# Queueing later weight conversions behind the work at hand in an attention and two-layer-pair kernel

## The chip, the cores and the metric

One core of a Trainium2 chip runs the whole program. The metric is the device time of one execution in microseconds (us), as a median of several runs. TensorE (PE) does the matrix products, VectorE (DVE), ScalarE (ACT) and GpSimd (POOL) the elementwise work, and one DMA queue on SyncE (SP) issues all transfers. Each engine takes its own instructions in the order of the program.

## The reference

```
attn:  a = softmax(causal(q k^T / 8)); local = a v
       mem = (phi(q) M_prev) / (phi(q) z_prev + 1e-6), phi(x) = elu(x) + 1
       x = sigmoid(beta) mem + (1 - sigmoid(beta)) local     # 2304 tokens x 512
moe :  h = x w_in;  x = (h * cos(h)) w_out                   # 512 -> 2048 -> 512
moe2:  h = x w_in;  out = (h * tanh(softplus(h))) w_out      # 512 -> 2048 -> 512
```

Queries, keys and values are 4 x 8 x 576 x 64, and all data of the two feed-forward pairs come as 8-byte words (float64).

## The kernel before, in words

Every product of the two feed-forward pairs is made of three: each operand is split into a rounded high part H and a rest L, and H·H, H·L and L·H are added in PSUM. So each value that enters a product first costs a cast (`scaled`) and a subtraction.

The weights come as 8-byte words. `fetch` (L133) loads 512 of them for each partition into a tile `wst` (4 buffers); `to_f32` turns them into float32: a rescaling of the upper word (`scaled("ws")`, L129 when GpSimd does it), a conversion of the lower word on ScalarE (L140) and two shift-and-merge steps on VectorE (L141, L142). Then comes the cast (L125 on ScalarE, L129 on GpSimd) and the subtraction. A **conversion** below is all of this for one `wst`. The table `TURNS` says which engines take which kind of step in turn.

The stages, by the time of the profile:

1. **Attention** (0 to 380 us), with the first half of the first pair's weights converted beside it, and the first pair's first half (`ffn` with blocks of 256 tokens, 36 units) from about 130 us to 472 us. In its tail, after attention is over, `load_half` converts the second half of the first pair's weights: 16 conversions (`gb`).
2. **First pair, second half** (472 to 690 us): `ffn` with blocks of 512 tokens, again 36 units, which come in twos. For two units: L422 products into `h`; L376 and L377 (the argument of the cosine), L381 (sin on ScalarE, both units at once), L384 (h·cos), the cast of `g` and the subtraction L394 on GpSimd; one pair later the L481 products into `y`. At the end of a block L504 adds the partial sum from DRAM (`yp`, loaded by L503) and L505 stores it to `ysF`. Beside it `strassen_weights` converts the second pair's weights: 16 conversions for `w_in` with sums of sub-blocks (L533), their H and L parts (L537) and stores to `wsD`; then 16 for `w_out`, kept on chip as `wo`. `strassen_x` forms the sums of the first 768 tokens (`xr` to `xc`, stored in `xsD`).
3. **Second pair, by Strassen's scheme** (690 to 1081 us): 24 groups, three blocks of 768 tokens by eight slices `tl` of the hidden dimension. A group k makes seven products A11, S2, A12, S3, S1, A22, S4 (L625, six matmuls each) from seven `wq` tiles (10 buffers) and seven `xc` tiles into two PSUM banks; a copy of the first product (`x1`, L675, ScalarE) and sums (L638, VectorE) turn them into four outputs, each with Mish on ScalarE (L642), a cast and a subtraction (L645) into `g3`. The L656 products of group k-1 (36 matmuls into `y`) stand between the products of group k. In group 6 and 14 the sums for the next 768 tokens are started (`coming`).

The order on each engine is set by a scheduler that works from the order in which the code is traced and from its own estimates. `tc.issue_after(ins)` puts every instruction that is traced inside it, on `ins`'s engine, behind `ins` in that engine's order; it sets an order and adds no semaphore. Without it the scheduler may put a conversion for a later group ahead of work at hand.

## Time and profile before

| what | us |
|---|---|
| median of 3 runs | 1083.99 (1081.04 to 1084.61) |
| the profiled execution | 1082.9 |
| its span, first to last instruction | 1081.1 |
| TensorE busy | 1034.7 |
| VectorE / ScalarE / GpSimd busy | 555.2 / 506.3 / 469.9 |
| mean granted TensorE clock | 0.982 of full speed |

A row of the timeline gives the start, the length, engine, line, operation, tiles and number of matmuls, and in brackets how long the engine was idle before it and who ended that. The waits group such idle times by who ended them. A table by windows gives the busy time of each engine in a stretch, the granted clock (1.00 is 2.4 GHz, 0.50 is 1.2 GHz) and the DMA engines' share.

### The profile page before, as it was taken

What the parts mean: (1) busy time and instruction counts of PE and PEld (TensorE: products, weight loads), DVE (VectorE), ACT (ScalarE), POOL (GpSimd) and SP (SyncE); (2) the same over time, 40 slices, a digit from 0 to 9 for tenths busy, and PEclk for the clock granted to TensorE, in tenths of its full rate; (3) what the DMA queues carried; (4) which work ended last, traced back from release to release, by engine and by line L of the source; (5) the groups of instructions that cost most, each with busy time, mean ns of one, the idle gap of its engine ahead of it and who ended that gap; (6) DMA issues with size and microseconds to landing.
All of it is one profiled execution on the core that took longest, in us unless ns stands there. A gap on an engine that the chain in (4) does not pass through costs nothing.

```text
span 1081.1 us, 18069 instructions
## 1 busy us (share of the span) xinstructions
PE 1034.7 (96%) x6560; PEld 890.6 (82%) x6560; DVE 555.2 (51%) x1214; ACT 506.3 (47%) x1102; POOL 469.9 (43%) x469
## 2 busy tenths in 40 slices
PE   6988999999999999899999999889999999999998
PEld 3756788787878899898888778778988889888987
DVE  4699864545555469725767856672224222322221
ACT  5886675555555544315445444433235233432323
POOL 3489633333333257615777996461126111511111
PEclk8999999999999999899999999889999999999999
DMA  7467323323221195414677795983436434454431
GB/s 258 163 224 244 123 90 102 119 88 95 86 75 54 43 340 189 156 47 145 219 285 301 254 341 203 394 307 117 125 111 219 117 110 135 127 173 120 118 88 59
DMA packets 88712, 177.36 MB, mean 164 GB/s; under 512 B 8240, under 2 KB 29232, under 8 KB 87600
## 3 DMA queue, kind: packets, MB, share of 16 engines
q1 hardware_dynamic: 88624, 176.21, 48.6%
q8 instruction: 52, 0.85, 0.3%
q14 instruction: 36, 0.29, 0.1%
HBM read 132.40 MB, written 43.78 MB: 163 GB/s over the span
## 4 chain that ended last, share of the span: by engine, by line
PE 77%; DMA 6%; POOL 5%; DVE 5%; ACT 3%; issue 3%; SPq 0%; ACTq 0%; DVEq 0%; POOLq 0%
PE y L656 18%; PE h L625 15%; PE h L422 15%; PE y L481 15%; PE o L333 4%; PE tp L306 3%; PE sp L247 3%; DVE wst L141 2%; PE o L322 1%; PE mp L286 1%; DVE wst L142 1%; DMA qd<-in_qT_dram 1%; DMA wq<-wsD 1%; POOL at L274 1%; POOL wst L129 1%
## 5 line engine op out<-in xcount | busy, mean ns | idle before, releaser
L481 PE MATMUL y<-g,w 128*128 128x256 f32 (+1 forms) x1344 | 226.4, 323 | 16.0 <-POOL g L394 7.0
L481 PEld LDWEIGHTS y<-g,w 128*128 128x128 f32 x1344 | 195.5, 196 | 43.8 <-issue 9.1
L656 PE MATMUL y<-wo,g 128*128 128x512 f32 x864 | 219.5, 395 | 4.1 <-ACT g L125 4.1
L422 PE MATMUL h<-xbH,w 128*128 128x256 f32 (+1 forms) x896 | 206.8, 317 | 0.0
L625 PE MATMUL h<-xc,wq 128*128 128x384 f32 x1008 | 197.2, 338 | 1.6 <-DMA wq<-wsD 1.0
L625 PEld LDWEIGHTS h<-xc,wq 128*128 128x128 f32 x1008 | 180.5, 189 | 12.4 <-DMA wq<-wsD 1.4
L656 PEld LDWEIGHTS y<-wo,g 128*128 128x128 f32 x864 | 161.9, 189 | 32.4 <-ACT g L125 4.4
L638 DVE TENSOR_TENSOR us<-h,us 128x384 f32<-128x384 f32 x120 | 66.8, 556 | 217.9 <-PE h L625 195.1
L645 POOL TENSOR_TENSOR g<-us,g 128x384 fp32r<-128x384 f32 x48 | 49.5, 1032 | 267.9 <-ACT g L125 253.8
L422 PEld LDWEIGHTS h<-xbH,w 128*128 128x128 f32 x896 | 151.0, 191 | 12.5 <-issue 1.0
L274 POOL TENSOR_SCALAR at<-at,sm,omg 128x128 f32<-128x128 f32 (+2 forms) x144 | 102.7, 723 | 128.3 <-DVE sm L272 109.7
L394 POOL TENSOR_TENSOR g<-u,g 128x512 fp32r<-128x512 f32 x72 | 102.5, 1439 | 126.5 <-DVE g L127 53.4
L422 PE MATMUL h<-xbL,w 128*128 128x256 f32 (+1 forms) x448 | 141.0, 315 | 0.0
L376 ACT ACTIVATE u<-h 128x512 int32<-128x512 f32 x72 | 42.4, 593 | 104.3 <-PE h L422 100.7
L422 PEld LDWEIGHTS h<-xbL,w 128*128 128x128 f32 x448 | 85.5, 191 | 5.4 <-issue 0.3
L252 ACT ACTIVATE at<-at,mn 128x128 f32<-128x128 f32 (+3 forms) x128 | 70.9, 555 | 27.1 <-DVE mn L249 25.6
L642 ACT ACTIVATE us<-us 128x384 f32<-128x384 f32 x72 | 37.7, 524 | 88.8 <-DVE us L638 88.7
L129 POOL TENSOR_SCALAR wst<-wst 128x512 f32<-128x512 f32 x64 | 52.7, 825 | 49.4 <-DMA wst<-in_w1i_dram 24.5
L141 DVE SCALAR_TENSOR_TENSOR wst<-wst 128x512 int32<-128x512 int32 x64 | 66.1, 1040 | 10.8 <-POOL wst L129 10.7
L377 DVE SCALAR_TENSOR_TENSOR u<-u,h 128x512 f32<-128x512 int32 x72 | 48.5, 680 | 43.2 <-ACT u L376 43.1
L142 DVE SCALAR_TENSOR_TENSOR wst<-wst 128x512 int32<-128x512 int32 x64 | 69.2, 1090 | 0.6
L306 PE MATMUL tp<-ident,at 128*128 128x128 f32 x384 | 62.6, 283 | 6.7 <-POOL at L274 5.5
(99 smaller groups left out, 1320.1 us busy)
## 6 DMA issues: line engine op xcount, KB each, us to landing
wq<-wsD SPq DMA_DIRECT2D x168, 256.0 KB, 3.0
wsD<-ws SPq DMA_DIRECT2D x8, 1792.0 KB, 7.8
wst<-in_w1i_dram SPq DMA_DIRECT2D x16, 512.0 KB, 4.7
wst<-in_w1o_dram SPq DMA_DIRECT2D x16, 512.0 KB, 5.6
wst<-in_w2i_dram SPq DMA_DIRECT2D x16, 512.0 KB, 4.5
wst<-in_w2o_dram SPq DMA_DIRECT2D x16, 512.0 KB, 6.0
xsD<-xc SPq DMA_DIRECT2D x7, 768.0 KB, 5.4
xc<-xsD SPq DMA_DIRECT2D x7, 768.0 KB, 9.0
```

Source lines behind the costliest of these rows:

```text
L129: eng.tensor_scalar(dst, src, scale, 1.0, ALU.mult, ALU.mult)
L141: nc.vector.scalar_tensor_tensor(lo, hi, -(1 << 31), lo, ALU.bitwise_and, ALU.bitwise_or)
L142: nc.vector.scalar_tensor_tensor(lo, hi, 3, lo, ALU.logical_shift_left, ALU.bitwise_or)
L252: marks["act"] = nc.scalar.activation(at[:, :N], at[:, :N], AF.Exp, bias=mn[:, j:j + 1], scale=-1.0, accum_out=sm[:, j:j + 1]).ins
L274: turn_of("sc", b == 0).tensor_scalar(at[:, :N], at[:, :N], sm[:, j:j + 1], gates[j], ALU.mult, ALU.mult)
L306: nc.tensor.transpose(tp[:, c:c + P], at[:, c:c + P], ident)
L394: turn_of(kind).tensor_tensor(gL, g, gH.bitcast(F32), ALU.subtract)
L422: nc.tensor.matmul(h[:, a * T:(a + 1) * T], w_[:, c, f0:f0 + P], x_[c], start=m == 0, stop=m == 3 * NC - 1)
L481: nc.tensor.matmul(y[e // per][:, cols], w_[:, f, es], g_, start=fst and m == 0 and e % per == 0, stop=lst and m == 2, skip_group_check=True)
L625: nc.tensor.matmul(b, w[:, wl, c], x[:, xl, c], start=first and m == 0, stop=m == 5, skip_group_check=True)
L638: nc.vector.tensor_tensor(c, b, x, ALU.add)
L656: nc.tensor.matmul(y[t], g[:, gl, t * P:(t + 1) * P], w_, start=tl == 0 and last == 0 and m == 0, stop=tl == ng - 1 and last == 1 and m == ...
```

## The change

Four edits that belong together, all in the second half of the program:

- **Tail of the first half, and the second half of the first pair.** The 16 conversions of `gb` come one for two steps from the start (before: all of the first six steps, then every second), each behind the last `marks["cos"]` (L384, VectorE) and the last sin (L381, ScalarE).
- **Fewer conversions of the second pair beside the first.** One for every fourth step rather than every third, so 1 of the 16 `w_out` conversions is done when Strassen's stage begins, where before it were 7 or more; in that stage `made_c` asks for 2k + 4 rather than 2k + 6.
- **In Strassen's stage** conversions and the sums for later tokens are traced under `behind()`, that is behind the last Mish (ScalarE), the last sum (VectorE), the last GpSimd subtraction and the last `wq` load (SP). The first group's `wq` loads are interleaved with the `xc` loads.
- **Engines.** The second pair's rescaling (`"ws2"`) and all its casts (`"wh2"`) go to ScalarE; before, GpSimd did all rescalings and half of the casts. The subtraction of the sums of tokens (`"x3l"`) goes to GpSimd and VectorE in turn.

```diff
-    wh="ap", aT="av", yl="p", ml="vp", y0="v", y1="a", aD="v", y3="a", x3l="p", x3d="v", ws4="p",
+    wh="ap", aT="av", yl="p", ml="vp", y0="v", y1="a", aD="v", y3="a", x3l="pv", x3d="v", ws4="p", ws2="a", wh2="a",
...
+    def load_w(tl, n):
+        t = wk.tile([P, 2, 2, P], F32R, tag="wq", name="wq", bufs=BUFS["wq"])
+        marks["s"] = nc.sync.dma_start(t.rearrange("p l c f -> p (l c f)").bitcast(F32), wsD[tl, :, SLOT[n]]).ins
+        return t
+
+    def load_sums(x, w):
         for n in PROD:
+            w[n] = load_w(0, n)
             x[n] = wk.tile([P, 2, 2, TS], F32R, tag="xc", name="xc", bufs=BUFS["xc"])
...
+    def behind():
+        es = ExitStack()
+        for e in "avps":
+            if e in marks:
+                es.enter_context(tc.issue_after(marks[e]))
+        return es
...
-            next(coming, None)
+            with behind():
+                next(coming, None)
...
-            if i < 2 * AHEAD or i % 2 == 0:
-                done_b = next(gb, done_b)
+            if i % 2 == 0:
+                with tc.issue_after(marks["cos"]), tc.issue_after(last_sin[0]):
+                    done_b = next(gb, done_b)
...
             while done_b < min(4 * ((i + 2) // 4 + 1), 4 * NTL) - 1:
-                done_b = next(gb)
+                with tc.issue_after(marks["cos"]), tc.issue_after(last_sin[0]):
+                    done_b = next(gb)
...
-            if i % 3 == 1:
+            if i % 4 == 1:
                 with tc.issue_after(marks["cos"]), tc.issue_after(last_sin[0]):
                     made_c = next(gc, made_c)
...
-        for k in strassen_ffn(b_pools[0], wo2, xs):
-            while made_c < min(2 * k + 6, DFF // P):
-                made_c = next(gc)
+        for k in strassen_ffn(b_pools[0], wo2, xs, w0):
+            while made_c < min(2 * k + 4, DFF // P):
+                with behind():
+                    made_c = next(gc)
```

How it moves instructions, at three places. VectorE in the tail of the first half, before, from the cosine products of two units (27 and 28, L384) to the next two's; `wst` is a conversion in work, `g` what the L481 products wait for:

```order
L384 TENSOR_TENSOR u_5292<-h_5303,u_5292 128x512
L178 TENSOR_TENSOR w112_4924<-wst_5295,w102_4923 128x512
L127 CAST g_5332<-u_5292 128x512
L141 SCALAR_TENSOR_TENSOR wst_5365<-wst_5365 128x512
L127 CAST g_5336<-u_5292 128x512
L142 SCALAR_TENSOR_TENSOR wst_5365<-wst_5365 128x512
L141 SCALAR_TENSOR_TENSOR wst_5429<-wst_5429 128x512
L142 SCALAR_TENSOR_TENSOR wst_5429<-wst_5429 128x512
L377 SCALAR_TENSOR_TENSOR u_5422<-u_5422,h_5397 128x512
L178 TENSOR_TENSOR w132_4926<-wst_5429,w122_4925 128x512
L141 SCALAR_TENSOR_TENSOR wst_5497<-wst_5497 128x512
L142 SCALAR_TENSOR_TENSOR wst_5497<-wst_5497 128x512
```

The same two units with the change:

```order
L384 TENSOR_TENSOR u_5268<-h_5279,u_5268 128x512
L141 SCALAR_TENSOR_TENSOR wst_5137<-wst_5137 128x512
L127 CAST g_5308<-u_5268 128x512
L141 SCALAR_TENSOR_TENSOR wst_5205<-wst_5205 128x512
L127 CAST g_5312<-u_5268 128x512
L142 SCALAR_TENSOR_TENSOR wst_5137<-wst_5137 128x512
L142 SCALAR_TENSOR_TENSOR wst_5205<-wst_5205 128x512
L178 TENSOR_TENSOR w111_4920<-wst_5205,w101_4919 128x512
L377 SCALAR_TENSOR_TENSOR u_5398<-u_5398,h_5373 128x512
L377 SCALAR_TENSOR_TENSOR u_5398<-u_5398,h_5413 128x512
```

Two conversions stand between two pairs of units instead of four, and the two L377 of the next pair follow each other.

ScalarE from the last outputs of Strassen's group 0 to the first of group 1, before; `us_7827` is the copy `x1` of group 1, `us_7855` its first Mish, `xc_8641` a sum for the next 768 tokens:

```order
L642 ACTIVATE us_7799<-us_7799 128x384
L125 ACTIVATE g3_7802<-us_7799 128x384
L675 ACTIVATE us_7827<-h_7819 128x384
L140 ACTIVATE wst_8081<-wst_8081 128x512
L140 ACTIVATE wst_8089<-wst_8089 128x512
L125 ACTIVATE wo012_6012<-wst_8089 128x512
L642 ACTIVATE us_7855<-h_7819 128x384
L571 ACTIVATE xc_8641<-xt_8639 128x768
L125 ACTIVATE g3_7857<-us_7855 128x384
```

The same place with the change; L648 is the Mish and L681 the copy:

```order
L648 ACTIVATE us_7751<-us_7751 128x384
L125 ACTIVATE wst_7335<-wst_7335 128x512
L140 ACTIVATE wst_7335<-wst_7335 128x512
L125 ACTIVATE wst_7429<-wst_7429 128x512
L140 ACTIVATE wst_7429<-wst_7429 128x512
L125 ACTIVATE g3_7754<-us_7751 128x384
L125 ACTIVATE wst_7578<-wst_7578 128x512
L140 ACTIVATE wst_7578<-wst_7578 128x512
L681 ACTIVATE us_7803<-h_7795 128x384
L125 ACTIVATE wo01_5972<-wst_7335 128x512
L125 ACTIVATE wo02_5974<-wst_7429 128x512
L648 ACTIVATE us_7831<-h_7795 128x384
```

The sum for later tokens is gone from between Mish and cast, and six conversion steps stand ahead of the copy of group 1.

TensorE where the first pair ends, with the change; `xc_7478` and `wq_7476` are the operands of A11 of group 0, `g_7414` belongs to unit 70 and `g_7541` to unit 71 of 72:

```order
L481 MATMUL y_7553<-g_7414,w121_4921 128x256 x2
L481 MATMUL y_7553<-g_7414,w131_4922 128x256
L630 MATMUL h_7683<-xc_7478,wq_7476 128x384 x6
L481 MATMUL y_7552<-g_7541,w122_4925 128x256
L481 MATMUL y_7553<-g_7541,w122_4925 128x256
```

Before, all 48 L481 products of units 71 and 72 stood ahead of the first L625 product; now A11 of group 0 stands ahead of them, and most of S2 in their middle.

## Rows read from the trace of the kernel before

**Rows 1.** The page: the span, and TensorE's busy time.
```profile
span 1081.1 us, 18069 instructions
PE 1034.7 (96%) x6560; PEld 890.6 (82%) x6560; DVE 555.2 (51%) x1214; ACT 506.3 (47%) x1102; POOL 469.9 (43%) x469
```

**Rows 2.** Table by windows: length, busy us of each engine (instructions), clock, DMA share, GB/s.
```profile
430.00:452.00 22.00, 19.04 (x135) 18.54 (x134) 20.57 (x25) 8.82 (x13) 17.15 (x16) 0.84 0.50 158
...
600.00:660.00 60.00, 54.89 (x250) 44.59 (x249) 40.81 (x45) 25.79 (x40) 56.10 (x45) 1.00 0.79 288
...
724.00:1050.00 326.00, 325.46 (x1619) 292.66 (x1618) 86.42 (x152) 112.95 (x214) 74.93 (x60) 1.00 0.44 131
```

**Rows 3.** Waits of PE from 430 to 452 us: total us, times, longest.
```profile
PE y L481 <- DVE yp L127: 1.7, 1, 1.7
PE y L481 <- POOL g L394: 1.3, 1, 1.3
```

**Rows 4.** Waits of PE from 600 to 660 us.
```profile
PE y L481 <- POOL g L394: 5.1, 4, 1.9
```

**Rows 5.** Waits of PE from 660 to 724 us.
```profile
PE y L656 <- ACT g L125: 4.1, 1, 4.1
PE y L481 <- ACT g L125: 3.2, 1, 3.2
PE h L625 <- DMA wq<-wsD: 1.0, 1, 1.0
PE y L481 <- POOL g L394: 0.6, 1, 0.6
```

**Rows 6.** Timeline of PE: start, length, line, tiles, matmuls, idle before.
```profile
427.64 5.92 PE L481 MATMUL y<-g,w 128*128 128x256 f32 x48
...
443.41 7.70 PE L481 MATMUL y<-g,w 128*128 128x256 f32 x42 [1.68 <-DVE yp L127]
...
663.89 3.63 PE L481 MATMUL y<-g,w 128*128 128x512 f32 x15
...
682.39 8.16 PE L481 MATMUL y<-g,w 128*128 128x256 f32 x46 [0.61 <-POOL g L394]
...
716.28 2.93 PE L656 MATMUL y<-wo,g 128*128 128x512 f32 x6 [4.06 <-ACT g L125]
...
724.20 1.55 PE L656 MATMUL y<-wo,g 128*128 128x512 f32 x6
```

**Rows 7.** Groups of DVE from 486 to 690 us, by form: busy, mean ns.
```profile
L142 DVE SCALAR_TENSOR_TENSOR wst<-wst 128x512 int32<-128x512 int32 x25 | 32.4, 1313 | 0.3
L141 DVE SCALAR_TENSOR_TENSOR wst<-wst 128x512 int32<-128x512 int32 x25 | 30.1, 1219 | 3.4 <-POOL wst L129 3.4
```

**Rows 8.** Groups of POOL from 486 to 690 us, by form.
```profile
L394 POOL TENSOR_TENSOR g<-u,g 128x512 fp32r<-128x512 f32 x36 | 54.3, 1526 | 36.6 <-ACT g L125 33.0 <-issue 3.6
L129 POOL TENSOR_SCALAR wst<-wst 128x512 f32<-128x512 f32 x22 | 17.3, 790 | 14.6 <-DMA wst<-in_w2i_dram 9.4 <-DMA wst<-in_w2o_dram 3.7 <-DVE wst L142 1.3
```

**Rows 9.** Timeline of ACT from 655 to 735 us.
```profile
676.71 1.15 ACT L381 ACTIVATE u<-u,c_hpi 128x1024 f32<-128x1024 f32 x1 [2.73 <-DVE u L377]
...
678.43 1.28 ACT L798 ACT_TABLE_LOAD   x1
...
706.21 1.24 ACT L140 ACTIVATE wst<-wst 128x512 int32<-128x512 uint32 x2
```

**Rows 10.** Landing times of L503, the loads of yp.
```profile
DMA to landing us min/median/max: 2.9/4.6/10.0
```

**Rows 11.** Landing times of L603, the loads of xc.
```profile
DMA to landing us min/median/max: 4.4/9.0/12.8
```

**Rows 12.** Table by windows, the stretch of the saturated DMA engines.
```profile
676.00:712.00 36.00, 31.11 (x166) 28.26 (x164) 25.31 (x33) 15.85 (x27) 17.79 (x16) 0.91 1.02 394
```

**Rows 13.** Groups of ACT from 690 us on, by form.
```profile
L642 ACT ACTIVATE us<-us 128x384 f32<-128x384 f32 x72 | 37.7, 524 | 88.8 <-DVE us L638 88.7
```

**Rows 14.** Groups of DVE from 690 us on, by form.
```profile
L579 DVE TENSOR_TENSOR xt<-xr,xt 128x768 f32<-128x768 f32 x2 | 3.5, 1771 | 2.2 <-DMA xr<-ysF 2.2
```

More of the change, by code (lines that the diff above doesn't have):

```diff
@@ L134, in fetch, with to_f32 @@
         return st
-    def to_f32(st):
+    def to_f32(st, kind="ws"):
         lo, hi = st[:, :, 0], st[:, :, 1]
-        scaled("ws", hi.bitcast(F32), hi.bitcast(F32), REBIAS)
+        scaled(kind, hi.bitcast(F32), hi.bitcast(F32), REBIAS)
         nc.scalar.activation(lo, lo.bitcast(U32), AF.Copy, scale=LOW * 2.0 ** -29, bias=0.2495)
@@ L516, in ahead @@
                 raw[i + AHEAD] = fetch(srcs[i + AHEAD])
-            yield to_f32(raw.pop(i)) if i >= 0 else None
+            yield to_f32(raw.pop(i), "ws2") if i >= 0 else None
     def strassen_weights(win, wout):
@@ L535, in sums @@
             for k0, k1, t in ((0, 2, pc[1]), (2, 3, pc[0][:, 0:1]), (3, 7, sw)):
-                scaled("wh", ws[:, k0:k1, 0], t)
+                scaled("wh2", ws[:, k0:k1, 0], t)
                 turn_of("w2l").tensor_tensor(ws[:, k0:k1, 1], t, ws[:, k0:k1, 0].bitcast(F32), ALU.subtract)
@@ L551, in gen @@
                         dH, dL = tiles[n - n_in]
-                        scaled("wh", dH, t)
+                        scaled("wh2", dH, t)
                         turn_of("w3l").tensor_tensor(dL, t, dH.bitcast(F32), ALU.subtract)
@@ L597, in strassen_x @@
         halves("S4", b22)
-    def load_sums(x):
+    def load_w(tl, n):
[3 more added lines that the diff above has]
+    def load_sums(x, w):
         for n in PROD:
+            w[n] = load_w(0, n)
             x[n] = wk.tile([P, 2, 2, TS], F32R, tag="xc", name="xc", bufs=BUFS["xc"])
@@ L604, in load_sums, with strassen_ffn @@
             yield n
-    def strassen_ffn(pool, wo, xs):
+    def behind():
[4 more added lines that the diff above has]
+        return es
+    def strassen_ffn(pool, wo, xs, w):
         ng = DFF // (2 * P)
@@ L611, in strassen_ffn @@
         ys = {}
-        def load_w(k):
-            w = {}
-            for n in PROD:
-                t = wk.tile([P, 2, 2, P], F32R, tag="wq", name="wq", bufs=BUFS["wq"])
-                nc.sync.dma_start(t.rearrange("p l c f -> p (l c f)").bitcast(F32), wsD[groups[k][1], :, SLOT[n]])
-                w[n] = t
-            return w
         def product(b, x, w, first):
@@ L637, in add @@
             c = cell()
-            nc.vector.tensor_tensor(c, b, x, ALU.add)
+            marks['v'] = nc.vector.tensor_tensor(c, b, x, ALU.add).ins
             return c
         def act(src, dst):
-            nc.scalar.activation(dst, src, AF.Mish)
+            marks['a'] = nc.scalar.activation(dst, src, AF.Mish).ins
             g = wk.tile([P, 2, TS], F32R, tag="g3", name="g3", bufs=BUFS["g3"])
             scaled("mh", g[:, 0], dst)
-            turn_of("ml").tensor_tensor(g[:, 1], dst, g[:, 0].bitcast(F32), ALU.subtract)
+            ins = turn_of("ml").tensor_tensor(g[:, 1], dst, g[:, 0].bitcast(F32), ALU.subtract).ins
+            marks['p' if ins.engine == mybir.EngineType.Pool else 'v'] = ins
             return g
@@ L666, in strassen_ffn @@
         g = {}
-        w = load_w(0)
         for k in range(n + 1):
@@ L674, in strassen_ffn @@
                 x1 = cell()
-                nc.scalar.activation(x1, A, AF.Copy)
+                marks['a'] = nc.scalar.activation(x1, A, AF.Copy).ins
                 product(B, x["S2"], w["S2"], True)
@@ L701, in strassen_ffn @@
                 if k + 1 < n:
-                    w = load_w(k + 1)
+                    w = {n: load_w(groups[k + 1][1], n) for n in PROD}
                 if groups[k][1] == ng - 2 and k + 2 < n:
@@ L706, in strassen_ffn @@
                     coming = strassen_x(nt, xs[nt])
-                    next(coming)
+                    with behind():
+                        next(coming)
             if k > 0:
@@ L772, in attention_moe_moe_kernel @@
     gx = strassen_x(0, {}, True)
-    xs = {0: {}}
-    gl = load_sums(xs[0])
+    xs, w0 = {0: {}}, {}
+    gl = load_sums(xs[0], w0)
     with tc.issue_after(marks["sp"]):
@@ L799, in attention_moe_moe_kernel @@
     with tc.issue_after(table), tc.issue_after(marks[large[-2]]):
-        for k in strassen_ffn(b_pools[0], wo2, xs):
-            while made_c < min(2 * k + 6, DFF // P):
-                made_c = next(gc)
+        for k in strassen_ffn(b_pools[0], wo2, xs, w0):
+            while made_c < min(2 * k + 4, DFF // P):
+                with behind():
+                    made_c = next(gc)
 _OUTS = [((2304, 512), "float32")]
```

## The prediction

> **What bounds the kernel now.** First the page: TensorE is busy for 1034.7 of 1081.1 us [rows 1], so a gain can come only from the 46 us in which it stands, or from stretches in which it runs at half clock. Then the table by windows, to see where these lie. From 724 to 1050 us TensorE is busy for 325.46 of 326.00 [rows 2]: nothing is to be had there, and whatever the change queues there can only lose. Other windows with holes (attention, the last store) lie outside the change. So I read the waits of TensorE and its timeline in the three places before 724 us; the reader is to see who ended each wait, and what the first matmuls after it cost.
>
> The clock is granted at 1.00 of 2.4 GHz in full stretches and at 0.50 (1.2 GHz) for a while after a long hole. The timeline shows it as slower matmuls: 48 took 5.92 us ahead of the hole of 1.68, and 42 took 7.70 behind it [rows 6]. At 5.92 / 48 = 0.123 each, 42 would take 5.2, so the half clock cost 2.5. The 46 behind the hole of 0.61 (which follows one of 3.2 [rows 5]) took 8.16 instead of 5.7: again 2.5. The first six behind the hole of 4.06 took 2.93, where six later took 1.55; I give this place 2.5 too, an estimate by the other two. The holes of up to 1.9 at 600 to 660 us left the clock at 1.00 [rows 2, 4].
>
> The bill of the kernel before, in us:
> - **A**, tail of the first half, 430 to 452: 1.7 + 1.3 [rows 3] + 2.5 = 5.5.
> - **B**, first pair's second half, 600 to 660: 5.1 in four holes, all ended by GpSimd's subtraction [rows 4].
> - **C**, the last units of the first pair: 3.2 + 0.6 [rows 5] + 2.5 = 6.3; **D**, the wait for `wq`: 1.0 [rows 5].
> - **E**, first products of `y` in Strassen's stage: 4.1 [rows 5] + 2.5 = 6.6.
>
> Together 24.5. All else keeps its time.
>
> **A: fewer conversions for a pair of units.** VectorE is busy for 20.57 of 22.00 us [rows 2]: it is the bound there. A conversion costs it 1.22 + 1.31 = 2.53 [rows 7]; a pair of units lasts TensorE 96 × 0.123 = 11.8, so the window holds nearly two pairs. Two conversions fewer for each pair take 2 × 2 × 2.53 = 10.1 off 20.57. VectorE then has half its time free, and the cast of `g` comes in time. −5.5, all of it. The other end: if one hole of 1.3 stays, without a cold stretch, plus another as long, −2.9. No conversions come short later: sixteen, two for each pair, need eight pairs, and the eighteen pairs of the stage have them.
>
> **B: GpSimd.** It is busy for 56.10 of 60.00 us [rows 2]. It loses the 22 rescalings (17.3 us of the 204 from 486 to 690) [rows 8] and, with the casts, more; conversions are begun every fourth step and not every third. Of 60 us this frees 60 × 17.3 / 204 = 5.1 by the rescalings, and a quarter of the remaining conversion work. The subtraction needs 36 × 1.53 = 54.3 us of those 204, and it is what TensorE waits for. −5.1; the other end, half of it, −2.5, if bursts of casts and of `x3l` still stand ahead of a subtraction. What takes over, ScalarE, was busy for 25.79 of 60 [rows 2]; its new steps (0.62 each, half of the 1.24 for two) [rows 9] add two for each conversion.
>
> **C and D: the end of the first pair.** I count from the end of the last product of the second-last layer half, 663.89 + 3.63 = 667.5 on the old time [rows 6], as 0. Ahead of A11 of group 0 TensorE now has 96 matmuls, 11.8 us. Its operands and the last `g` come by this chain: the fourth L504 waits for its `yp`, which is loaded after the first store: 1.5 (an estimate: the store's share of the 4.6) + 4.6 [rows 10] = 6.1. Behind it come the add and two L377, some 2.1 on VectorE (an estimate, by the 1.2 to 1.3 of L141 and L142 [rows 7]), so 8.2. Then on ScalarE the sin 1.15, two conversion steps 1.24, the table load 1.28 and the cast 0.6 [rows 9]: 12.5, some 0.5 more for the handing over, 13. Then the subtraction 1.53 [rows 8]: 14.5. The `xc` loads are issued at some 8.6 and land 4.4 later at the least [rows 11], at 13.0. So TensorE waits 13.0 − 11.8, about 1.4 with the sums, and then 0.9 for the subtraction: 2.3. Neither is as long as the holes that brought the half clock. Then the DMA: seven `xc` of 0.79 MB and seven `wq` of 0.26 MB make 7.3 MB; at 394 GB/s, the rate of the saturated stretch [rows 12], that is 18.6 us, so that S4's operands are there at about 29, where TensorE wants them at 28: 1.0. Left are 3.3 of 7.3: −4.0. The ends: nothing gained (the chain takes the place of the old wait, cold stretch and all), and −7.3.
>
> Of the table load the Trainium skill, "ScalarE: Activation LUTs", section "What ACT_TABLE_LOAD costs", says that a drain of about 1.38 us goes with each load. The row has 1.28 for the load and shows no drain; by the page the last `g` would come 1.4 later and C and D would give −2.6 rather than −4.0. I keep to the row.
>
> **E: group 1 of Strassen's stage.** Before, TensorE waits 4.1 there for a `g` that stood on ScalarE behind copies, conversions and a sum for later tokens. Now the sum is gone, but six conversion steps stand between the last Mish of group 0 and the copy `x1` of group 1, as the order shows. A12 of group 1 needs `x1`. After the end of S4 of group 0: the sum 0.6 (estimate), the Mish 0.52 [rows 13], six steps 6 × 0.62 = 3.7 [rows 9], a cast and the copy, each like the Mish, 1.0: 5.8. TensorE has twelve matmuls of 384 in the meantime; at 3.63 / 15 = 0.242 for 512 [rows 6] that is 12 × 0.18 = 2.2. The hole is 3.6, of the length that brought the half clock: 3.6 + 2.5 = 6.1, against 6.6. −0.5: this is a stall that changes its place. The ends: −6.6, if GpSimd or DMA deliver these conversions so early that ScalarE does them during the waits of group 0; and +1. In group 2 the same chain has two steps (0.6 + 0.5 + 1.24 + 0.5 = 2.9) against TensorE's 9 × 0.24 + 2.2 = 4.4, and from group 3 on four steps (0.6 + 0.5 + 2.5 + 1.0 = 4.6) against 24 × 0.24 + 2.2 = 8.0: no holes.
>
> On these six steps the Trainium skill, same page and section, says that ACTIVATEs back to back overlap by about 93 ns. The row has 1.24 for two of 512 columns, which shows no overlap; by the page the six steps would take 0.5 less and the hole would be 3.1. I take the row.
>
> **F: group 6.** The sums for the next tokens (two L579 of 1.77 [rows 14], an L572, and two conversions of 2.53 [rows 7]) now all stand between the last sum of group 6 and the first of group 7 on VectorE: 3.5 + 1.5 (estimate) + 5.1 = 10.1, with the add 10.6 after S4 of group 6. TensorE has about 9.3 of work till then (an estimate: 30 matmuls of 512 and 12 of 384, 30 × 0.24 + 2.2). +1.3, between 0 and +6.5 (a hole of 4 with its cold stretch). Before, the window shows only 0.54 of holes in all.
>
> **Sum.** −5.5 − 5.1 − 4.0 − 0.5 + 1.3 = −13.8. The profiled execution took 1082.9, 1.1 below the median 1083.99. 1082.9 − 13.8 + 1.1 = 1070.2; I say **1070**.
>
> **Rivals.**
> 1. **ScalarE's queue holds nobody up** (E ends at its good end, C and D near theirs): the conversions are fetched early enough and ScalarE is idle in group 0. For it: ScalarE waits for the sums for most of this stage (88.8 us) [rows 13]. Against: the order is fixed, and DMA is saturated just then [rows 12], so the words come late. −17 to −24.5: **1059.5 to 1067**.
> 2. **GpSimd and VectorE stay late** (B −2.5, C and D 0 to −2, F +4): for it, the subtractions stand in GpSimd's queue behind casts in bursts, and the subtraction of the sums moves to it in part. Against: the 17.3 us that it loses. −4 to −11: **1073 to 1080**.
> 3. **The change doesn't do what it says**: fewer conversions early mean more late, each stall is only moved, 1080.7 to 1087, around **1083**. Against: TensorE has no free time in which a later engine is the bound except at the four places.
> 4. **Slower, by one mechanism**: A11 of group 0 now stands ahead of the last 48 L481 products, and TensorE takes its work in order. If the store lands in 10, `yp` in 10.0 [rows 10] and `xc` in 12.8 [rows 11], its operands come at 10.0 + 10.0 + 12.8 = 32.8, where before no product of the first pair waited for them. Then the hole is 32.8 − 11.8 = 21.0 and with 2.5 it is 23.5 in place of 7.3: +16.2, with the rest (−9.8) +6.4: **1090**. It decides from a landing at about 29, since 29 − 11.8 + 2.5 − 7.3 − 9.8 = +2.6; that takes every one of the loads at its slowest, while the medians give 4.6 and 9.0.
>
> **How the numbers follow.** Forecast, 1067 to 1073: 0.42. Rival 1: 0.20. Rival 2: 0.22. Rival 3: 0.09. Rival 4: 0.07. About 0.3%, 3.3 us, is what a measurement of this kernel can tell from no change. So faster (below 1080.7) has 0.42 + 0.20 + 0.22 = 0.84, the same 0.09, slower 0.07. The range is 1060 to 1081: it holds the forecast, rival 2 and nearly all of rival 1.
>
> **What the next profile would show.** A: no wait between L481 and its cast in the tail, VectorE half busy, clock 1.00 there. B: no waits of L481 for the L394 subtraction between 600 and 660, GpSimd some 45 of 60. C and D: a wait of A11 for `xc` or `wq` of 1 to 2 us, and a wait of S4 of about 1. E: a wait of a product of group 1 for a copy on ScalarE of about 3.6, with slow matmuls behind it, and ScalarE busy with conversions ahead of it. F: a wait of about 1 in group 7, by VectorE. Outside these places the busy share of TensorE stays as it is, and the mean clock is above 0.982. I am wrong if `xc` lands late (rival 4 or the bad end of C and D), if the copy of group 1 is in time (rival 1), or if GpSimd is still the bound of B.

## The result, and the profile after

The changed kernel takes 1068.1 us (median of 4 runs, 1066.67 to 1070.39); the kernel before takes 1083.55 over the runs beside it. The ratio is 0.9863, with an interval of 0.9838 to 0.9888. The forecast was 1070, in a range of 1060 to 1081. The profiled execution, at 1070.39 the longest of the four, has a span of 1068.6 us, against 1081.1 [rows 1]:

```profile
span 1068.6 us, 18074 instructions
...
PE 1031.4 (97%) x6560; PEld 888.7 (83%) x6560; DVE 559.0 (52%) x1224; ACT 532.5 (50%) x1154; POOL 417.5 (39%) x407
```

The stage ahead of the change also differs a little from one program to the next: the same matmul at 206 us starts up to 4 us earlier or later in the programs of this study. So I compare from that matmul to the last products of `y`. These are the two rows of the kernel before, from TensorE's timeline, and behind them the same two of the kernel after:

```profile
205.54 5.78 PE L481 MATMUL y<-g,w 128*128 128x256 f32 x46 [1.39 <-ACT aT L125]
...
1070.11 6.32 PE L656 MATMUL y<-wo,g 128*128 128x512 f32 x27
```

```profile
207.49 5.78 PE L481 MATMUL y<-g,w 128*128 128x256 f32 x46 [1.39 <-ACT aT L125]
...
1057.56 6.32 PE L663 MATMUL y<-wo,g 128*128 128x512 f32 x27
```

864.57 us became 850.07: 14.5 less, where the prediction had 13.8 (the medians differ by 15.45). The table by windows of the kernel after answers to [rows 2]; its columns are the length, the busy time of PE, PEld, DVE, ACT and POOL, the clock, the DMA share and GB/s:

```profile
430.00:452.00 22.00, 22.00 (x186) 22.00 (x185) 16.78 (x21) 8.07 (x13) 14.46 (x13) 1.00 0.40 120
600.00:660.00 60.00, 60.00 (x306) 51.39 (x305) 37.77 (x48) 31.99 (x50) 38.94 (x30) 1.00 0.78 280
724.00:1050.00 326.00, 321.50 (x1585) 288.90 (x1584) 114.56 (x176) 124.18 (x235) 76.10 (x57) 0.99 0.47 140
```

In the first two windows TensorE has no hole left and GpSimd, which was full in the second (56.10), is busy for 38.94. In the third, where there was nothing to gain, 4 us of holes are new. TensorE's timeline, with the idle time ahead of each row in brackets, has every hole above 0.3 us that remains in the stretches which the change touches:

```profile
667.76 1.28 PE L630 MATMUL h<-xc,wq 128*128 128x384 f32 x6 [0.46 <-DMA xc<-xsD]
...
683.40 1.28 PE L630 MATMUL h<-xc,wq 128*128 128x384 f32 x6 [0.96 <-DMA wq<-wsD]
685.36 1.31 PE L630 MATMUL h<-xc,wq 128*128 128x384 f32 x6 [0.67 <-DVE us L644]
687.26 1.28 PE L630 MATMUL h<-xc,wq 128*128 128x384 f32 x6 [0.60 <-DMA wq<-wsD]
690.05 2.29 PE L630 MATMUL h<-xc,wq 128*128 128x384 f32 x6 [1.50 <-ACT us L681]
692.13 2.17 PE L663 MATMUL y<-wo,g 128*128 128x512 f32 x6
...
797.33 4.21 PE L630 MATMUL h<-xc,wq 128*128 128x384 f32 x12 [4.23 <-DVE us L644]
801.33 2.18 PE L663 MATMUL y<-wo,g 128*128 128x512 f32 x6
```

The first row is A11 of group 0, the second S4 of group 0, then A11, S2 and A12 of group 1. The rows at 690.05, 692.13, 797.33 and 801.33 run at half clock: six of 384 take 2.29 rather than 1.28, twelve 4.21 rather than 2.27, six of 512 take 2.17 and 2.18 rather than 1.55.

The bill beside the prediction's, in us:

| place | before | forecast of the change | after: holes + half clock | change |
|---|---|---|---|---|
| A tail of the first half | 5.5 | −5.5 | 0 | −5.5 |
| B second half | 5.1 | −5.1 | 0 | −5.1 |
| C, D end of the first pair | 7.3 | −4.0 | 0.46 + 0.96 | −5.9 |
| E group 1 | 6.6 | −0.5 | 0.67 + 0.60 + 1.50 + 1.6 | −2.2 |
| F group 7 | 0 | +1.3 | 4.23 + 2.6 | +6.8 |
| sum | 24.5 | −13.8 | | −11.9 |

The table misses 2.6 of the 14.5. Most of it is that an idle time is shorter than the delay that goes with it. I compare the start of the same matmul in both traces. From ahead of A's two holes to behind them the kernel before loses 3.5 us, where the idle times add up to 2.95; the half clock behind them costs 2.5, as the prediction had it. The four holes of B, 5.1 us of idle time, go with 6.4 us. C, D and E together give 8.6 rather than 8.1, and F costs 0.4 less than the table says. The likely reason is the row of the last matmul ahead of a hole: a matmul of 256 by itself has a row of 0.28 to 0.35 us, while in a run the next one starts after 0.12, so that part of the delay counts as busy. No run tests this reading.

### The profile page after: what moved, and what is told of

Its sections match the earlier page's. It is cut to its first block, busy times and chain, and to the rows that moved or that the text cites. A ratio compares the mean times of both kernels' runs of the same rounds, so it can differ in the third digit from the quotient of the medians.

```text
span 1068.6 us, 18074 instructions
## 1 busy us (share of the span) xinstructions
PE 1031.4 (97%) x6560; PEld 888.7 (83%) x6560; DVE 559.0 (52%) x1224; ACT 532.5 (50%) x1154; POOL 417.5 (39%) x407
## 5 line engine op out<-in xcount | busy, mean ns | idle before, releaser
L481 PE MATMUL y<-g,w 128*128 128x256 f32 (+1 forms) x1344 | 219.8, 317 | 4.2 <-ACT aT L125 4.2
L481 PEld LDWEIGHTS y<-g,w 128*128 128x128 f32 x1344 | 191.0, 190 | 29.5 <-issue 9.1
L651 POOL TENSOR_TENSOR g<-us,g 128x384 fp32r<-128x384 f32 x48 | 51.9, 1080 | 289.1 <-ACT g L125 282.1
L644 DVE TENSOR_TENSOR us<-h,us 128x384 f32<-128x384 f32 x120 | 66.7, 556 | 175.1 <-PE h L630 174.5
L394 POOL TENSOR_TENSOR g<-u,g 128x512 fp32r<-128x512 f32 x72 | 105.5, 1481 | 123.8 <-DVE g L127 45.1
L648 ACT ACTIVATE us<-us 128x384 f32<-128x384 f32 x72 | 37.7, 524 | 102.0 <-DVE us L644 99.4
L142 DVE SCALAR_TENSOR_TENSOR wst<-wst 128x512 int32<-128x512 int32 x64 | 72.4, 1142 | 0.6
L377 DVE SCALAR_TENSOR_TENSOR u<-u,h 128x512 f32<-128x512 int32 x72 | 48.7, 681 | 43.5 <-ACT u L376 43.1
L333 PE MATMUL o<-aT,vt 128*64 128x128 f32 (+1 forms) x896 | 67.4, 276 | 2.0 <-ACT aT L125 2.0
L249 DVE CUSTOM_DVE_ANT_0 at<-sp,mask 128x128 f32<-128x128 f32 (+3 forms) x128 | 59.1, 482 | 19.4 <-PE sp L247 11.8
```

What stands on the lines that cost most here:

```text
L142: nc.vector.scalar_tensor_tensor(lo, hi, 3, lo, ALU.logical_shift_left, ALU.bitwise_or)
L249: nc.vector.tensor_tensor_reduce(at[:, :N], sp[:, :N], mask[:, SM - q0:SM - q0 + N], SSC, 3.0e38, ALU.add, ALU.min, mn[:, j:j + 1])
L333: marks["pe"] = nc.tensor.matmul(o[j * D:(j + 1) * D, :n], st["vt"][:kk, c, j * D:(j + 1) * D], a, start=False, stop=c == i, skip_group_ch ...
L394: turn_of(kind).tensor_tensor(gL, g, gH.bitcast(F32), ALU.subtract)
L481: nc.tensor.matmul(y[e // per][:, cols], w_[:, f, es], g_, start=fst and m == 0 and e % per == 0, stop=lst and m == 2, skip_group_check=True)
L644: marks['v'] = nc.vector.tensor_tensor(c, b, x, ALU.add).ins
```

## The experiments

Each kernel was timed beside the kernel before, and one execution of it was profiled. The first four make a part of the change alone, on the kernel before; the others undo or change a part in the changed kernel. Two parts were never run by themselves: the first `wq` loads between the `xc` loads, and `x3l` on GpSimd and VectorE in turn. What each of these two is worth is not known.

### The tail alone

Only the first of the two edits on the first pair's conversions, on the kernel before:

```diff
-            if i < 2 * AHEAD or i % 2 == 0:
-                done_b = next(gb, done_b)
+            if i % 2 == 0:
+                with tc.issue_after(marks["cos"]), tc.issue_after(last_sin[0]):
+                    done_b = next(gb, done_b)
```

> The kernel before with the edit of the tail of the first half alone (conversions for the second half of the first pair one for two steps, behind the last L384 and the last sin). Theory: the tail is bound by VectorE's four conversions for each pair of units, so the waits of L481 between 430 and 452 us (1.7 and 1.3) and the half clock behind them go, 5.5 us, and the other places keep their waits: ratio 0.995. Rival: the conversions that are now later burden the stage behind; then the waits of L481 for GpSimd (5.7 in all from 600 on) begin earlier and grow by 2 or more, and the ratio is 0.997 to 1.001.

1090.89, ratio 1.0066 (1.0047 to 1.0085): slower, a miss for the theory and beyond the rival. The tail's own waits are gone, but where the second half begins the timeline shows new ones, this one and two more at 493 and 495 us (0.86 and 1.30):

```profile
479.19 0.80 PE L481 MATMUL y<-g,w 128*128 128x256 f32 x2 [2.93 <-DVE g L127]
```

The conversions which the tail no longer makes come there, and since that code didn't yet put them behind, two L141 (2.37 us) stand ahead of the cast of `g`. At the start of Strassen's stage the waits grow too, from 5.1 us to 6.9. The change has a second edit for these conversions, which this kernel leaves out.

### Both edits on the first pair's conversions

```diff
             while done_b < min(4 * ((i + 2) // 4 + 1), 4 * NTL) - 1:
-                done_b = next(gb)
+                with tc.issue_after(marks["cos"]), tc.issue_after(last_sin[0]):
+                    done_b = next(gb)
```

> The kernel before with both halves of the edit on the conversions of the first pair: one for two steps and behind the last L384 and sin in the tail, and also those that are still open in the second half traced behind them (the run of the tail alone left these as before, and had waits of 2.9 and 3.1 us with half clock between 479 and 570). Theory: it was these later conversions, put ahead of work at hand, that cost what the tail gave; with them behind it, A's 5.5 is a net gain: the waits between 470 and 600 are gone and the ratio is 0.994 to 0.997. Rival: it is their mere amount beside the second half, whose GpSimd rescalings come on top of those for the second pair; then L394's waits stay above 5 from 470 on and the ratio is 1.001 or more.

1081.86, ratio 0.9989 (0.9972 to 1.0006): no difference that the interval shows. The waits at 479 to 495 are gone, but TensorE's waits between 470 and 700 us are now more than in the kernel before (14.6 us in place of 9.9). The two largest (total, times, longest):

```profile
PE y L481 <- POOL g L394: 5.7, 5, 1.6
PE y L481 <- DVE yp L504: 3.6, 2, 3.1
```

L394's share is what it was before (5.7); what is new is the waits for VectorE and a later `wq`. So both were partly right: A's 5.5 come free, and what comes later takes them back. That the put-off conversions are the cause of each of these waits is likely, not shown. Alone, this part is worth nothing that the interval shows.

### The change of engines alone

`ws2="a", wh2="a"` with the two calls that use them, on the kernel before.

> The kernel before with the change of engines for the second pair's weights alone (rescaling and all casts on ScalarE; the sums for later tokens stay on GpSimd). Theory: GpSimd is the bound between 600 and 660 us, so the waits of L481 for L394 there (5.1) are gone and GpSimd is busy for some 40 of the 60 us; A keeps its 5.5; E, the wait for ScalarE at the first products of group 0, grows from 4.1 by the two or more extra steps of 0.6 that ScalarE gets there, to 5 to 7: in all -2 to -4, ratio 0.996 to 0.998. Rival: it is the rate of the conversions that frees GpSimd; then more than 2.5 of the 5.1 stay and the ratio is 1.000 to 1.003.

1073.87, ratio 0.9916 (0.9898 to 0.9934), about 10 us: more than the theory gave it. The waits from 470 to 700 us, and below them from 700 on:

```profile
PE y L481 <- POOL g L394: 3.5, 5, 0.9
...
PE y L656 <- ACT g L125: 2.4, 1, 2.4
```

L394's waits fell from 5.7 to 3.5 with none above 0.94, and the 3.2 ahead of the last units to 1.0: the last `g` had been late through GpSimd too. The wait of E shrank from 4.1 to 2.4, where I had expected that ScalarE's extra steps make it longer. By the same matmuls in both traces, 4.0 us were won up to the end of the last full block (656 us in the kernel before) and 6.0 behind it, in C, D and E.

### The smaller count alone

`i % 4` for `i % 3` and `2 * k + 4` for `2 * k + 6`, on the kernel before.

> The kernel before with the smaller count of conversions alone (every fourth step beside the first pair; in Strassen's stage 2k+4 asked for rather than 2k+6). Theory: B shrinks from 5.1 to 2 to 3, since GpSimd loses a quarter of the conversions there; the last two conversions now stand in VectorE's queue beside the sums of group 6, so a wait of a product of group 7 for L638 appears, as in the changed kernel (4.2 and the half clock, 6.8 in all); E grows, since nothing is queued behind: net +2 to +8, ratio 1.002 to 1.007. Rival: the wait in group 7 comes from tracing behind the work at hand, not from the count; then there is none here and the ratio is 0.996 to 1.000.

1083.99, ratio 1.0004 (0.9993 to 1.0015): nothing. L394's waits were 4.4 in two, and a wait of 5.84 for VectorE (L638) stood at 719 us, in an early group. In group 7 there was none, as the rival had it: without being put behind, the last conversions are drawn into earlier groups. So the smaller count by itself doesn't bring the wait of F.

### The engines undone

The changed kernel with `ws2="p", wh2="ap"`.

> The changed kernel with the old engines for the second pair's weights: rescaling on GpSimd, casts on GpSimd and ScalarE in turn. Theory: L481 waits for L394 again between 500 and 690 us, 2 to 5 us in all (with the smaller count alone 4.4 were left, with the new engines alone 3.5), and A11 and the last g come later behind GpSimd's queue, 2 to 3; in return three steps fewer stand ahead of the copy of group 1, and E's wait of 1.5 and half clock go, 3: net +1 to +5, 1069 to 1073, ratio 0.987 to 0.991. Rival: with the smaller count GpSimd has room enough and E's gain is all that is seen: 1064 to 1067, ratio 0.982 to 0.985.

1078.3, ratio 0.9945 (0.9927 to 0.9963): 10 us lost, outside both expectations. TensorE's waits from 470 to 700 us, and below them from 700 to 830:

```profile
PE h L630 <- DMA wq<-wsD: 3.5, 1, 3.5
...
PE y L481 <- POOL g L394: 1.5, 3, 0.8
...
PE y L663 <- POOL wo L129: 2.5, 1, 2.5
```

L394 is the smaller part of what comes back (1.5). A11 of group 0 waits 3.5 for its first `wq`, whose load SP issued at 666.19 us and not at 660.33 (why it was issued later, these traces don't settle), and a product of `y` waits 2.5 for the cast of `wo` in GpSimd's queue. E's wait for the copy stays at 1.5, although only three conversion steps stand ahead of it now; and in group 7 TensorE waits 3.0 for a Mish and 1.9 for a cast, where the changed kernel waits 4.2. The profiled execution is the longest of six, 1080.5.

### The tail undone

The changed kernel with the old two edits on the first pair's conversions.

> The changed kernel with the old order of the first pair's conversions (all of the first six steps of the tail, then every second; those left over not put behind). Theory: A's waits of 1.3 and 1.7 and the half clock are back, 5.5, and the second half gains nothing, since it has no waits of L481 left: 1073.5, ratio 0.991. Rival: the conversions that are done earlier free VectorE and GpSimd for more of the second pair's, which helps the start of Strassen's stage: 1070 or less.

1073.59, ratio 0.9902 (0.9888 to 0.9917), 5.5 above the changed kernel, which is what A was priced at. The old holes (1.28 and 1.68) are back with the half clock:

```profile
443.44 7.88 PE L481 MATMUL y<-g,w 128*128 128x256 f32 x42 [1.68 <-DVE yp L127]
```

That it is 5.5 to the tenth is chance: by the same matmuls in both traces the tail loses 6.2, and F is smaller here (3.03 in place of 4.23). Within the change, then, A is a net gain; alone it was none. What makes the difference is probably the room that the engines' edit gives in the second half, where L394's waits are 0.28 us in all; the tail together with that edit alone was not run.

### No conversions in group 6

The changed kernel with one line changed, so that group 6 has sums for later tokens and no conversions:

```diff
-            while made_c < min(2 * k + 4, DFF // P):
+            while made_c < (4, 6, 8, 11, 14, 16)[min(k, 5)]:
```

> The changed kernel with one edit: the conversions asked for in Strassen's stage are 4, 6, 8, 11, 14, 16 after groups 0 to 5 rather than 2k+4, so that none is left for the end of group 6, where the sums for the next tokens begin. Theory: two conversions on VectorE (5.8 us from the first L141 to the last L142 in the changed kernel) stand between the last sum of group 6 and the first of group 7, so that sum comes some 6 us earlier, the wait of 4.2 in group 7 and its half clock (2.6) go, and the time is 1068.1 - 6.8 = 1061, ratio to the kernel before 0.980. Rival: the sums themselves are slowed by GpSimd's work beside them (an L572 took 1.78 on VectorE) and by the landing of xr (1.9 of waits); then a wait of 2 to 4 stays with its half clock, 1065 to 1068.

1066.99, ratio 0.9845 (0.9824 to 0.9866), 3.4 us less in the profiled span. The direction is the theory's, and the half clock in group 7 is gone; by the same matmuls some 5 us are won in that place. But the median's gain of 1.1 is within what the intervals (0.9838 to 0.9888 for the changed kernel) can't tell from none. The changed kernel was profiled in its longest execution; how large F is in the other three, no trace shows. In group 7 waits of 0.20, 0.78 and 0.36 are left, of which the longest:

```profile
794.22 2.37 PE L630 MATMUL h<-xc,wq 128*128 128x384 f32 x12 [0.78 <-DVE us L644]
```

VectorE's work there is still uneven: an L579 takes 2.60 beside GpSimd's L589 (787.42 to 789.26), where one took 0.96 just before.

```profile
787.48 2.60 DVE L579 TENSOR_TENSOR xt<-xr,xt 128x768 f32<-128x768 f32 x1
```

The changed kernel holds a second comparison. In its group 14 the sums for the last 768 tokens are put behind in the same way, and no conversions are left: in group 15 TensorE waits only 0.27, for a Mish, as it did before the change.

### The sums' GpSimd work on VectorE

The changed kernel with `x3l="v"` and L589 and L594 on VectorE, which also takes this work from GpSimd in the first pair's second half; the two conversions stay in group 6.

> The changed kernel with all elementwise work of the sums for later tokens that GpSimd does (L572, L589, L594) given to VectorE; the two conversions stay in VectorE's queue in group 6. In the changed kernel two L141 took 4.56 us there beside GpSimd's L589 and L572, and 0.69 each where GpSimd was idle. Theory (VectorE is slowed by GpSimd's work beside it): without that work L141, L142 and L572 take 0.7 to 1.0 each, the eleven instructions ahead of the first sum of group 7 make about 9.0 us, and the wait falls from 4.2 to 2 or less: F costs 2 to 4 rather than 6.8, ratio to the kernel before 0.982 to 0.985. Rival (it is only the length of the queue): one L589 and one or two L572 of 1.8 to 2.5 come on top of 13.6 us, the wait grows to 7 or more, ratio 0.989 or above.

1066.71, ratio 0.9852 (0.9839 to 0.9865), 5.0 less in the profiled span; by the medians the gain is 1.4, which the intervals don't tell from none either. VectorE has more instructions ahead of the first sum of group 7 than in the changed kernel, and is done sooner. The changed kernel, VectorE (the last row is that sum):

```profile
785.57 0.96 DVE L579 TENSOR_TENSOR xt<-xr 128x768 f32<-128x768 f32 x1 [1.25 <-DMA xr<-ysF]
...
787.60 0.96 DVE L579 TENSOR_TENSOR xt<-xr,xt 128x768 f32<-128x768 f32 x1 [0.60 <-DMA xr<-ysF]
788.47 1.78 DVE L572 TENSOR_TENSOR xc<-xr,xc 128x768 fp32r<-128x768 f32 x1
790.17 4.56 DVE L141 SCALAR_TENSOR_TENSOR wst<-wst 128x512 int32<-128x512 int32 x2
794.65 1.28 DVE L142 SCALAR_TENSOR_TENSOR wst<-wst 128x512 int32<-128x512 int32 x2
...
796.73 0.55 DVE L644 TENSOR_TENSOR us<-h,us 128x384 f32<-128x384 f32 x1
```

GpSimd's work beside it:

```profile
789.40 2.56 POOL L589 TENSOR_TENSOR xr<-xr 128x768 f32<-128x768 f32 x1
791.92 2.26 POOL L572 TENSOR_TENSOR xc<-xt,xc 128x768 fp32r<-128x768 f32 x1
```

The experiment, VectorE, where GpSimd had only one instruction, from 788.27 to 789.77:

```profile
788.21 2.11 DVE L141 SCALAR_TENSOR_TENSOR wst<-wst 128x512 int32<-128x512 int32 x2
...
793.19 0.54 DVE L644 TENSOR_TENSOR us<-h,us 128x384 f32<-128x384 f32 x1
```

The two L141 take 4.56 beside two GpSimd instructions, 2.11 beside one; one alone takes 0.69. The wait falls from 4.23 to 0.79 and the half clock goes. That is not all GpSimd's: `xr` landed earlier here, and the 1.85 us that VectorE waits for it in the changed kernel are gone. From the end of S4 the sum is ready 3.4 us sooner: 2.4 by the L141 and 1.9 by `xr`, less 0.9 for the added instructions with the shorter L572 counted in. So two things make F, the conversions in the queue and GpSimd's work beside them, and a late `xr` adds to it. No conversions there (the run before this one) is enough to end the half clock, and so is this run's lighter GpSimd with the earlier `xr`; what GpSimd's work is worth without the change of `xr` is read from the rows, not tested.

### Fewer conversions behind group 0

As the kernel with no conversions in group 6, but with 3, 5, 8, 11, 14, 16, so that two are put behind group 0 rather than three.

> The changed kernel with conversions asked for as 3, 5, 8, 11, 14, 16 after groups 0 to 5: none in group 6, and two rather than three after group 0, so that four ScalarE steps rather than six stand ahead of the copy of group 1. Theory: F as with 4, 6, 8, 11, 14, 16 (waits of 2.1 in all in place of 4.2 and the half clock), and the wait for the copy of group 1 falls from 1.5 to 2.0 to below 1, with no half clock behind it (1.6): 1064, ratio 0.982. Rival: E's copy does not wait for the steps but for A11's own end or for the clock; then the wait and the half clock stay and the time is that of the other, 1067.

1068.25, ratio 0.9867 (0.9854 to 0.9879): no gain, a miss. The wait for the copy is still 1.46 in group 1, and stands now in groups 2 and 3 too:

```profile
688.12 1.32 PE L630 MATMUL h<-xc,wq 128*128 128x384 f32 x6 [1.46 <-ACT us L681]
705.64 1.32 PE L630 MATMUL h<-xc,wq 128*128 128x384 f32 x6 [1.71 <-ACT us L681]
723.89 2.27 PE L630 MATMUL h<-xc,wq 128*128 128x384 f32 x6 [2.33 <-ACT us L681]
```

The last row is at half clock; in group 1 the half clock is gone. The conversions which group 0 is spared burden the next ones. In group 1 the copy does come sooner, 3.7 us after the start of group 0's last sum rather than 5.3, but TensorE has waited less on its way there (0.9 in place of 2.2) and is there sooner by nearly as much.

### Conversions not put behind

The changed kernel, with this alone undone:

```diff
             while made_c < min(2 * k + 4, DFF // P):
-                with behind():
-                    made_c = next(gc)
+                made_c = next(gc)
```

> The changed kernel, but the conversions of Strassen's stage are traced without being put behind the work at hand (the sums for later tokens still are). Theory: by the order the conversions then stand ahead of the Mish of group 0 on ScalarE and are over before group 6: the wait of 4.2 in group 7 goes (-5 to -7), and at the first outputs of group 0 a wait of a product of y for ScalarE is back, 2 to 5 us with the half clock, in place of E's 3.8: in all 1063 to 1068, ratio 0.981 to 0.985. Rival: the words land late since DMA is saturated, the Mish of group 0 waits for them, and the wait is 6 or more: ratio 0.986 or above.

1060.72, ratio 0.9797 (0.9784 to 0.9810): the fastest kernel here, 7.4 us below the changed one and better than both expectations. E and all but 0.8 of F are gone. TensorE's two largest waits from 660 to 800 us:

```profile
PE y L481 <- POOL g L394: 0.9, 1, 0.9
PE h L630 <- DVE us L644: 0.8, 2, 0.5
```

ScalarE's timeline shows where the conversions went: from 666 to 676 us, into the time in which, in the changed kernel, it waited 7.34 for TensorE.

```profile
666.33 0.68 ACT L125 ACTIVATE wst<-wst 128x512 f32<-128x512 f32 x1
...
675.54 0.68 ACT L125 ACTIVATE wst<-wst 128x512 f32<-128x512 f32 x1 [0.71 <-DMA wst<-in_w2o_dram]
```

And TensorE gets other work in its own order: products of `y` stand between those of group 0, and there is no wait for `wq` left in that group.

```profile
678.47 1.67 PE L663 MATMUL y<-wo,g 128*128 128x512 f32 x6
679.98 1.21 PE L630 MATMUL h<-xc,wq 128*128 128x384 f32 x6
681.02 0.86 PE L663 MATMUL y<-wo,g 128*128 128x512 f32 x3
```

### Nothing put behind in Strassen's stage

The same, and the sums for later tokens are not put behind either.

> The changed kernel with nothing put behind the work at hand in Strassen's stage: neither conversions (as in the run before this, 1060.7) nor the sums for later tokens. By the order, the sums of the next tokens are pulled forward on VectorE. Theory: the sums were what the tracing behind was good for; next to GpSimd an L579 or L572 takes 2 to 2.6 us on VectorE and on ScalarE an L571 0.8, so ahead of the work at hand they bring waits of 1 to 4 us in the first groups: 1063 to 1067, ratio 0.982 to 0.986. Rival: the scheduler puts them where the engines have room, as it did with the conversions: 1059 to 1061.5, ratio 0.978 to 0.981.

1066.24, ratio 0.9844 (0.9829 to 0.9860): the theory's range, 5.5 above the run before. TensorE waits for `wq` (0.99 and 1.33) and for a subtraction on VectorE. Behind that it runs at half clock: 18 matmuls take 4.96, where 18 took 3.37.

```profile
688.05 3.37 PE L630 MATMUL h<-xc,wq 128*128 128x384 f32 x18 [1.33 <-DMA wq<-wsD]
...
699.35 0.96 PE L662 MATMUL y<-wo,g 128*128 128x512 f32 x3 [1.93 <-DVE g L650]
700.15 4.96 PE L630 MATMUL h<-xc,wq 128*128 128x384 f32 x18
```

In this kernel SP issues the four `xr` loads at 680 to 689 us, among the last `wq` loads, while the DMA engines are saturated (share 1.02 from 660 to 692). That these loads are what delays `wq` is likely, not shown by itself. So to put things behind costs 7.4 for the conversions, and pays 5.5 for the sums once the conversions are not put behind.

### The old count, conversions not put behind

The fastest kernel with `i % 3` and `2 * k + 6`.

> The changed kernel without the conversions put behind (1060.7) and with the old count: every third step beside the first pair, 2k+6 in Strassen's stage. Theory: GpSimd no longer rescales, but ScalarE and VectorE carry a third more conversions beside the first pair, and DMA more words: waits of L481 of 1 to 3 us come back between 600 and 690, nothing is won later: 1062 to 1065, ratio 0.981 to 0.984. Rival: fewer words are fetched while DMA is saturated at the start of Strassen's stage and fewer conversions stand in the first groups; then 1058 to 1060.5, ratio 0.977 to 0.980.

1070.46, ratio 0.9880 (0.9858 to 0.9901); the theory's direction, 10 us and not 2 to 4. TensorE waits for VectorE in the second half (L504 2.6, L384 2.4, both with conversions ahead of them) and for L394 1.7. The profiled execution is the shortest of six (1067.13, the others up to 1075.9), so it holds only part of the 10. The smaller count, worth nothing alone, is worth that much here.

## Why the prediction was right, and where it was not

**A** held: no hole is left in the tail, and undoing it costs 5.5. Its sentence that no conversions come short later was wrong as a reason: alone, this edit gained nothing or lost 7, by new waits in the second half. It is a net gain only beside the rest of the change.

**B** held in size, and in its rule that GpSimd is the bound; GpSimd is busy for 38.94 of the 60 us, where I had 45. But its weights were off: the change of engines alone gave 10 and not 5, for it also brought the last `g`, `wq` and `wo` earlier, which the prediction had put under C and E; undone, it costs 10. The terms of the sum are not independent, and only their sum came out.

**C and D** held step by step, and ended better (−5.9 for −4.0). With the end of the last full block's products, 655.8, as 0, A11 could begin at 11.5 (forecast 11.8), `xc` landed at 12.0 (13.0), the last subtraction ended at 14.8 (14.5), and S4 waited 0.96 for `wq` (1.0). A11 waited 0.46, where I had 1.4 (13.0 − 11.8 is 1.2). The step that failed is the wait of 0.9 for that subtraction: I took it as wanted right behind A11, but the products of the unit before stand in between (26 matmuls, 3.27 us), and five of S2.

I had set aside a drain beside the table load, and none shows: the load (1.28) begins 0.02 after the step ahead of it, and the two casts of `g` follow 0.02 after its end; the other loads of this trace behind its first are as tight. The Trainium skill, "ScalarE: Activation LUTs", section "What ACT_TABLE_LOAD costs", puts about 1.38 us for a drain beside each load; this trace disagrees.

```profile
664.85 0.68 ACT L140 ACTIVATE wst<-wst 128x512 int32<-128x512 uint32 x1
665.55 1.28 ACT L807 ACT_TABLE_LOAD   x1
666.85 1.15 ACT L125 ACTIVATE g<-u 128x512 fp32r<-128x512 f32 x2
```

**E** held as a mechanism: the copy `x1` of group 1 stands behind six conversion steps and TensorE waits for it.

```profile
685.74 0.66 ACT L125 ACTIVATE wst<-wst 128x512 f32<-128x512 f32 x1
...
688.97 0.65 ACT L140 ACTIVATE wst<-wst 128x512 int32<-128x512 uint32 x1
689.52 0.47 ACT L681 ACTIVATE us<-h 128x384 f32<-128x384 f32 x1
```

It was ready 5.3 after the end of S4 (684.7 to 690.0), where I had 5.8. The term that was too large is the hole: TensorE had lost 0.67 and 0.60 on the way there, so only 1.50 was left, and the half clock cost 1.6, not 2.5. I had taken the half clock for a matter of one long hole. Here it came after holes of 0.96, 0.67, 0.60 and 1.50 close behind each other, while a single hole of 1.9 at 651 us had left the clock at 1.00 before [rows 2, 4]. I had also misread a row. In [rows 9] two L140 take 1.24, which I took for "no overlap". In the changed kernel these steps start 0.55 to 0.58 apart (685.74, 686.31, 686.86, 687.44) and last 0.64 to 0.69 each: 1.24 is one start-to-start time and one whole length, each step overlaps the next by some 0.1, and six take 3.4. The Trainium skill, "ScalarE: Activation LUTs", section "What ACT_TABLE_LOAD costs", gives about 93 ns for that overlap; this trace agrees.

**F** is the term that was wrong, +6.8 for +1.3, just beyond the far end of its bounds (+6.5). The cover was right (9.4, forecast 9.3), but the sum was ready 13.5 after S4 rather than 10.6. The steps that failed: the two L141 at their mean of 1.22, where they took 2.28 each beside GpSimd; 1.85 of waits for `xr`, which I did not price; an L651 and a second L572 in the same queue, 1.4 together, which I had not counted; and the half clock, which I kept for the bound. That L142 and L579 were 1.4 and 1.8 shorter than by their means did not make up for it.

E and C came out better by 1.7 and 1.9 and F worse by 5.5, so that the places add up to 11.9; another 2.6 come from what the bill of the kernel before left out beside the idle times. A total of 13.8 for 14.5 is partly luck. Of the rivals, the first (ScalarE's queue holds nobody up) describes the kernel without the conversions put behind: 1060.72, in its span of 1059.5 to 1067. The fourth did not come near: A11 waited 0.46.

## What to carry to other kernels

"Behind the work at hand" is not safe by itself: work put behind the last instruction of one group is work put ahead of the first of the next, and where that next group has little cover it can be better done in the idle time before, as the conversions were here. Price work on an engine by what runs beside it, not by its mean over a stage. And parts of one change that shift work between the same engines need not have a fixed worth: the tail alone was worth nothing that could be measured and 5.5 in company, the count alone nothing and 10 in company (without the conversions put behind).

## What the runs showed of the hardware

VectorE was slowed by GpSimd, and only in some instructions. Those with both operands in SBUF vary widely over the changed kernel's run (each row: shortest, median and longest in ns), and those that read PSUM (L644, and L377 and L504 alike) hardly at all:

```profile
L141 DVE SCALAR_TENSOR_TENSOR wst<-wst x64: 673/686/2334, 58.8 to 792.4; 128x512 int32<-128x512 int32 x64
...
L644 DVE TENSOR_TENSOR us<-h,us x120: 539/557/558, 676.3 to 1057.8; 128x384 f32<-128x384 f32 x120
```

With no GpSimd instruction beside it, an L141 takes 0.68 to 0.70 (20 of them); beside GpSimd two took 2.11 with one, 4.56 with two. It looks like a wait rather than a slower rate: in group 6 the two L141 end 0.54 and 0.55 us after GpSimd's L589 and L572 do (at 792.50 and 794.73). In the run with the sums' GpSimd work on VectorE the first L141 starts 0.06 ahead of GpSimd's L651 and takes 0.69; the second ends 0.55 after that L651.

The Trainium skill, "SBUF — State Buffer", section "SBUF: two separate sides", has a rule for this: an instruction of VectorE with two SBUF inputs and a GpSimd instruction that reads SBUF take turns on a shared pair of ports, and whichever starts first holds it for the whole of its instruction. The trace agrees, as the ends of these L141 show. The prediction had not drawn on this.
